# A fused attention, gMLP and expert-attention kernel: the order of all work replaced, with fewer warm-up and filler products

## The chip, the cores and the metric

The kernel runs on one core of one Trainium2 chip. The metric is the device time of one launch in microseconds (us). A core has five engines that matter here: PE (TensorE) for products, DVE (VectorE), ACT (ScalarE) and POOL (GpSimd) for everything element by element, and SP (SyncE), from which this kernel issues every transfer (DMA). Each engine works through its own list of instructions in order; an instruction waits until what it reads is there and the buffer that it writes is free.

## What is computed

The reference, cut to what matters (B=4 batches, H=8 heads, S=576 positions, D=64, so 512 wide; E=4 experts):

```
def _attn_ref(q, k, v):                      # sliding window of 64
    scores = q @ k.T / sqrt(D), masked to 0 <= i - j < 64
    return softmax(scores) @ v
def _moe_ref(x, w_in, w_spatial, b_spatial, w_out):
    h = np.maximum(x @ w_in, 0.0)            # 512 -> 1024
    u, v = h[..., :512], h[..., 512:]
    v_n = (v - mu) / np.sqrt(var + 1e-06)
    v_s = np.einsum('ts,bsd->btd', w_spatial, v_n) + b_spatial
    return (u * v_s) @ w_out
def _moe2_ref(x, w_gate, wq, wk, wv, wo):    # the two best of 4 experts a position
    logits = x @ w_gate; topk, w = best two, softmax over them
    for e in range(E):
        q, k, v = x @ wq[e], x @ wk[e], x @ wv[e]
        ye = softmax(causal(q @ k.T / sqrt(Hd))) @ v @ wo[e]
        out += (weight of e in the best two, or 0) * ye
    return out
```

The result is `_moe2_ref(_moe_ref(_attn_ref(q, k, v)))`.

## The kernel before, in words

All matrices are split in two parts, a head (`xh`, `wh`, `qk`'s first half) and the rest (`xl`, `wl`), and a product of two matrices is three products of parts, so that nearly every result that PE leaves in PSUM is read twice: once by a copy to the head (line 415 on DVE, line 411 on ACT, through `copy`) and once by a subtraction for the rest (`sub`, line 424, on DVE or POOL).

Phase 1 runs the first two stages. `s_mm` (line 624) makes the window scores of two heads of a batch, DVE masks them (line 647), ACT takes the exponential (line 654), the probabilities are turned (`p_t`, line 681) or go through memory, and `pv` multiplies them by v. `prep64` (line 775) splits the loaded w_in in several steps on ACT, DVE and POOL; `b_v` (line 1017) and `b_u` (line 1096) multiply by its two halves, `b_mix` (line 1112) mixes positions. w_out is folded into wq, wk and wv (`prep_w2`, line 1266). Phase 2, from about 244 us, runs the experts in two pairs (`pr` 0 and 1) for each batch: `c_qk` (line 1430) makes q and k of a pair, the tile `qk` holds their heads and rests, `c_gate` (line 1512) picks the two best experts with 15 small operations on DVE (lines 1538 to 1552), scores are masked on DVE (lines 1641 and 1686), `c_pv` (line 1751) multiplies by v, `c_wo` (line 1798) by wo, and the output is stored.

Every piece of work is a node of a `Planner` (line 176). A node has a number, the engines on which it may run with a planned duration for each, and the nodes and buffers that it needs. Two tables fix everything: `ORDER` lists the node numbers in the order in which they are written into the program, and `ON` gives a digit for each, the engine (0 PE, 1 ACT, 2 DVE, 3 POOL, 4 SP). `run` walks the tables, so the planned durations, the start times in `free` and the landing of a DMA in `start` no longer decide anything once the tables stand; they served the search that made the tables. PSUM is a ring of 8 banks, and SBUF tiles are rings too, so a node can also wait for a buffer.

Two kinds of node compute nothing that is used: node 0 is a run of `WARM` products of a 128x128 tile of zeros, `hot`, at the start, and nodes 1 to 60 are fillers, one such product each, of which the tables list some. [...]

```
    warm = r_mm.new()
    def heat(n):
        for _ in range(n):
            mm(warm[:, :128], hot, hot)
    a = N((PE, 427.0 * WARM), lambda e: heat(WARM), alloc=[warm], prio=-1e9)
    for _ in range(FILL):
        N((PE, 228.0), lambda e: heat(1), [a], use=[warm], prio=1e9)
```

Of the kernel before, what the change touches and what calls it, by code (L numbers as in the profile page):

```python
# [1926 lines left out]
```

## Time and profile before

| | |
|---|---|
| median of 3 runs | 411.7 us (409.5 to 412.14) |
| the profiled execution | 408.59 us, of which the profile's span is 406.8 us |
| PE busy | 390.8 us, 96% of the span |
| DVE busy | 333.2 us, 82% |
| ACT, POOL busy | 208.8 and 209.9 us, 51 and 52% |
| moved by DMA | 72.45 MB, 178 GB/s on the mean |

Durations below come from the one profiled execution, which was 3.1 us faster than the median of the runs. An engine that is busy at nearly all times bounds the kernel only in the stretches in which the others wait for it, so the table is to be read together with the busy time by stretch.

### The profile page before, as it was taken

How to read it: one execution, taken by the hardware profiler on the slowest of the kernel's cores; microseconds unless marked ns; L12 is line 12 of the kernel's file. 1: busy time of each engine (PE TensorE's matmuls, PEld its weight loads, DVE VectorE, ACT ScalarE, POOL GpSimd, SP SyncE). 2: the span in 40 equal slices, each digit the busy share in tenths (PEclk: the TensorE clock that was granted, in tenths of full speed). 3: DMA queues.
4: the chain of work that ended last, by engine and by line, in shares of the span. 5: the costliest groups of instructions: out<-in, count | busy, mean ns of one | idle time of the engine just before them, and what ended most of it. 6: DMA issues, size and time to landing. Idle time of an engine off the chain costs nothing.

```text
span 406.8 us, 10676 instructions
## 1 busy us (share of the span) xinstructions
PE 390.8 (96%) x3678; PEld 346.3 (85%) x3678; DVE 333.2 (82%) x1213; ACT 208.8 (51%) x708; POOL 209.9 (52%) x278
## 2 busy tenths in 40 slices
PE   8798898999999999999999999999899989999996
PEld 7676688998799989998999999999689968896765
DVE  5998799879889868758747685899999999998852
ACT  4999786955296574321222141483573346354332
POOL 7787697455279545526371765355742255122400
PEclk9999999999999999999999999999999999999999
DMA  7999769679695855450220110028775977899874
GB/s 270 290 348 314 236 157 302 202 217 271 174 341 150 235 151 155 121 161 12 76 75 3 26 54 2 1 45 230 190 180 128 263 166 210 250 278 252 234 225 129
DMA packets 88410, 72.45 MB, mean 178 GB/s; under 512 B 15138, under 2 KB 80418, under 8 KB 88356
## 3 DMA queue, kind: packets, MB, share of 16 engines
q1 hardware_dynamic: 88356, 71.77, 61.3%
q8 instruction: 29, 0.48, 0.5%
q14 instruction: 25, 0.20, 0.1%
HBM read 47.89 MB, written 23.86 MB: 176 GB/s over the span
## 4 chain that ended last, share of the span: by engine, by line
PE 64%; DVE 23%; DMA 6%; ACT 3%; issue 3%; SPq 1%; POOL 0%; DVEq 0%; ACTq 0%
PE bank L400 63%; DVE p L1641 2%; DVE pa L647 2%; DVE p L1656 2%; DVE p L1686 2%; ACT pa L654 1%; DVE qk L424 1%; DMA qa<-in_qT_dram 1%; DMA d<-p 1%; SPq L506 1%; DMA pg<-d 1%; DMA kt<-in_kT_dram 1%; DMA dr<-pa 1%; DVE p L1653 1%; DVE pa L702 1%
## 5 line engine op out<-in xcount | busy, mean ns | idle before, releaser
L400 PE MATMUL bank<-xh,w 128*128 128x288 f32 x512 | 106.8, 296 | 0.4 <-DVE xl L424 0.4
L400 PEld LDWEIGHTS bank<-xh,w 128*128 128x128 f32 x512 | 83.5, 188 | 2.2 <-DVE xl L424 0.7
L400 PE MATMUL bank<-xl,w 128*128 128x288 f32 x256 | 75.4, 294 | 0.0
L400 PE MATMUL bank<-w,xh 128*128 128x512 f32 (+1 forms) x256 | 64.6, 342 | 0.1
L1653 POOL TENSOR_SCALAR p<-p,mg,fx 128x256 f32<-128x256 f32 (+3 forms) x45 | 27.7, 624 | 42.6 <-DVE ga L1539 10.0
L400 PEld LDWEIGHTS bank<-xl,w 128*128 128x128 f32 x256 | 48.1, 188 | 0.4
L400 PEld LDWEIGHTS bank<-w,xh 128*128 128x128 f32 x256 | 42.7, 188 | 5.2 <-ACT xh L411 0.3
L400 PE MATMUL bank<-w,xl 128*128 128x512 f32 (+1 forms) x128 | 43.3, 338 | 0.9 <-DVE xl L424 0.9
L1645 ACT ACTIVATE p<-p,mg 128x128 f32<-128x128 f32 (+3 forms) x56 | 30.9, 553 | 18.9 <-DVE mg L1641 10.6
L654 ACT ACTIVATE pa<-pa,mp 128x128 f32<-128x128 f32 x96 | 37.2, 391 | 2.2 <-issue 2.0
L647 DVE CUSTOM_DVE_ANT_0 pa<-bank,mask 128x128 f32<-128x128 f32 x120 | 28.4, 283 | 4.2 <-PE bank L400 4.1
L400 PE MATMUL bank<-qk 64*128 64x320 f32 (+4 forms) x288 | 27.7, 329 | 2.5 <-DVE qk L424 2.0
L400 PEld LDWEIGHTS bank<-qk 64*128 64x128 f32 x288 | 22.0, 185 | 6.8 <-ACT xh L411 1.8
L400 PEld LDWEIGHTS bank<-w,xl 128*128 128x128 f32 x128 | 24.1, 188 | 4.0 <-DVE xl L424 1.3
L1072 POOL TENSOR_TENSOR st<-st,nhalf 128x1 f32<-128x1 f32 (+1 forms) x20 | 14.2, 715 | 24.7 <-DVE st L1070 19.3
L1641 DVE CUSTOM_DVE_ANT_0 p<-bank,kmask 128x128 f32<-128x128 f32 (+3 forms) x56 | 25.1, 482 | 0.5
L424 POOL TENSOR_TENSOR vl<-vr,vh 128x512 fp32r<-128x512 f32 x14 | 19.2, 1374 | 11.0 <-ACT vh L411 10.7
L400 PE MATMUL bank<-pg,v 128*64 128x128 f32 (+2 forms) x224 | 23.9, 354 | 1.0 <-DVE qk L424 1.0
L400 PE MATMUL bank<-wsp_h,vh 128*128 128x288 f32 x80 | 24.0, 301 | 0.3 <-DVE mp L647 0.3
L400 PE MATMUL bank<-wsp_h,vl 128*128 128x288 f32 x80 | 23.6, 295 | 0.0
L400 PE MATMUL bank<-wsp_l,vh 128*128 128x288 f32 x80 | 23.6, 294 | 0.0
L1656 DVE STREAM_TRANSPOSE p<-p 128x768 f32<-128x768 f32 (+1 forms) x21 | 22.2, 1057 | 0.9 <-POOL p L1653 0.8
(277 smaller groups left out, 1053.6 us busy)
## 6 DMA issues: line engine op xcount, KB each, us to landing
vt<-in_v_dram SPq DMA_DIRECT2D x12, 512.0 KB, 5.8
dr<-pa SPq DMA_DIRECT2D x64, 96.0 KB, 3.1
pt<-dr SPq DMA_DIRECT2D x16, 384.0 KB, 4.7
d<-p SPq DMA_DIRECT2D x56, 96.0 KB, 2.0
qa<-in_qT_dram SPq DMA_DIRECT2D x44, 96.0 KB, 5.3
out_dram<-ot SPq DMA_DIRECT2D x15, 256.0 KB, 3.6
y<-in_w_in_dram SPq DMA_DIRECT2D x7, 512.0 KB, 6.3
d<-p SPq DMA_DIRECT2D x28, 128.0 KB, 3.0
```

Of the source, the lines that this page charges most:

```text
L400: pe.matmul(o, lhsT, rhs, start=start, stop=stop)
L424: engs[e].tensor_tensor(out=o, in0=a, in1=hi.bitcast(F32), op=ALU.subtract)
L506: nc.sync.dma_start(o, i)
L647: dve.tensor_tensor_reduce(out=at(j, e2), in0=sq(ps[:, j * 128:(j + 1) * 128]), in1=sq(mask(j)), scale=-0.125, scalar=3.0e38, op0=ALU.add, ...
L654: act.activation(at(j, e2), at(j, e2), AF.Exp, bias=mx[:, j, 0:1], scale=-1.0, accum_out=mx[:, j, 1:2])
L702: a = N((DVE, 902), lambda e: dve.transpose(pa.t, pa.t), [a], use=[pa], prio=prio, sbuf=True)
L1072: a = N((POOL, 560), lambda e: pool.tensor_tensor(out=st[:m, 9:10], in0=st[:m, 8:9], in1=nhalf[:m], op=ALU.pow), [n1], use=[st])
L1641: a = N((DVE, t_tt(L)), lambda _, ps=ps, c0=c0, L=L, I=I, e=e, n=n: dve.tensor_tensor_reduce(out=put(I, e), in0=as4(ps[:, c0:c0 + L]), in1 ...
L1645: done.append(N((ACT, 284 + 0.87 * L), lambda _, I=I, e=e, n=n: act.activation(put(I, e), put(I, e), AF.Exp, bias=mg[:, n, 0:1], scale=-1. ...
L1653: done.append(N({POOL: 328 + 0.832 * L, DVE: 190 + 0.52 * L}, lambda en, n=n, I=I, e=e: engs[en].tensor_scalar(put(I, e), put(I, e), mg[:, ...
L1656: a = N((DVE, 100 + 4.16 * w), lambda e: dve.transpose(P[:, :4 * w], P[:, :4 * w]), done, use=[P], prio=prio, sbuf=True)
L1686: dve.tensor_tensor_reduce(out=P[HALF[y], i * 320:(i + 1) * 320], in0=ps[y][HALF[y], :320], in1=tmask[HALF[y], 2 * i:2 * i + 2].rearrange( ...
```

## The change

`ORDER` and `ON` are replaced as a whole. The new order lists 1989 nodes, the old one 1996; the seven that are gone are fillers (11 before, 4 after), and `WARM` goes from 7 to 4. What PE multiplies is otherwise the same. By counting the nodes of the tables: 57 go from POOL to DVE, 39 from DVE to POOL, 66 from ACT to DVE, 64 from DVE to ACT, 18 from POOL to ACT and 16 from ACT to POOL; DVE has 871 nodes instead of 851, POOL 220 instead of 240, ACT 352 as before. The numbers of the planner that change with it (durations, start times, landings) do not reach the chip by themselves.

The diff, cut to its core (the first line of `ORDER` stands for both tables):

```diff
-WARM = 7
+WARM = 4
 ORDER = (
-    0, 12, 35, 61, 188, 62, 65, 58, 60, 189, 208, 196, 209, 21, 242, 241, 216, 298, 11, 78, 3, 190, 191, 192, 243, 197, 264, 244, 263, 85, 71, 210,
...
+    61, 0, 54, 27, 24, 62, 242, 65, 188, 208, 189, 241, 243, 263, 196, 264, 299, 209, 71, 298, 78, 68, 190, 191, 192, 64, 197, 216, 244, 265, 198, 251,
...
-        self.nodes, self.free, self.prio = [], [700.0, 2000.0, 2900.0, 7600.0, 560.0], 0.0
-        self.moved, self.data, self.cold, self.unit = [-1e9] * self.FLIGHT, 0.0, 5000.0, 0
+        self.nodes, self.free, self.prio = [], [1050.0, 2000.0, 2900.0, 7600.0, 560.0], 0.0
+        self.moved, self.data, self.cold, self.unit = [-1e9] * self.FLIGHT, 0.0, 1000.0, 0
...
-                self.moved.append(self.data + 250.0 + min(self.BEHIND, 1.2 * (self.data - t - self.WAY)))
+                self.moved.append(self.data + 450.0 + min(self.BEHIND, 1.2 * (self.data - t - self.WAY)))
...
-        S_N[n0] = S_N[n0 + 1] = top = N((PE, 654), s_mm, kn + [Q_N[n0], Q_N[n0 + 1], S_N.get(n0 - 1)], alloc=bank, use=hk, prio=prio,
+        S_N[n0] = S_N[n0 + 1] = top = N((PE, 680), s_mm, kn + [Q_N[n0], Q_N[n0 + 1], S_N.get(n0 - 1)], alloc=bank, use=hk, prio=prio,
...
-        n2 = N_(155, lambda: tt(out=gt(), in0=lf, in1=le, op=ALU.is_gt), [n1])
+        n2 = N_(270, lambda: tt(out=gt(), in0=lf, in1=le, op=ALU.is_gt), [n1])
```

Planned durations are also raised for the other gate operations, the power on POOL (560 to 680), two small operations of `b_v` and of the scores, one kind of `b_v` product and `c_pv` (651 to 760).

PE at the start of the program; a row is a line, an operation, what it writes and reads, its shape and how often it follows itself. `hot` is the tile of zeros, `vt` holds q and k of the first heads, a `bank` is one of PSUM's eight:

```order
 L1923 UNCONDITIONAL_BRANCH
-L400 MATMUL bank_68<-hot 128x128 x9
+L400 MATMUL bank_68<-hot 128x128 x7
 L400 MATMUL bank_69<-vt 64x128
 L400 MATMUL bank_70<-vt 64x128
```

Two products fewer stand ahead of the first scores; two between the first and the second scores, three behind the second and four further on are gone too, and one stands ahead of the first turned probabilities.

SP at the start, before (`in_w_in` is the weight w_in, whose loads to `prep64` go into `y`; `in_qT`, `in_kT` and `in_v` are what the attention reads):

```order
L506 DMA vt<-in_kq_dram 128x768 x2
L506 DMA ut_164<-in_kT_dram 128x4x256
L506 DMA qa<-in_qT_dram 128x192 x3
L506 DMA y_240<-in_w_in_dram 128x1024
L506 DMA qa<-in_qT_dram 128x192 x2
L506 DMA y_268<-in_w_in_dram 128x1024
L506 DMA y_270<-in_w_in_dram 128x1024
L506 DMA qa<-in_qT_dram 128x192
L506 DMA ut_164<-in_kT_dram 128x4x192
```

And in the change:

```order
L506 DMA y_248<-in_w_in_dram 128x1024
L506 DMA ut_164<-in_kT_dram 128x4x192
L506 DMA wol<-in_v_dram 128x2x256
L506 DMA qa<-in_qT_dram 128x192 x3
L506 DMA woh<-in_v_dram 128x2x256
L506 DMA qa<-in_qT_dram 128x192
L506 DMA kt<-in_kT_dram 128x576
L506 DMA woh<-in_v_dram 128x3x256
L506 DMA kt<-in_kT_dram 128x576
L506 DMA qa<-in_qT_dram 128x192 x2
L506 DMA y_479<-in_w_in_dram 128x1024
```

The first row of this is the second load of w_in and the last its third, which had stood next to the second: nine rows of the attention's loads have moved ahead of it. The later loads of w_in move back in the same way.

DVE where q and k of batch 1, second pair, are split, before (`qk_3464` is the tile of that pair; line 424 takes the rest of one piece out of its bank; `p`, `mc` are score tiles and their sums, `ga`, `gb` the gate's):

```order
L424 TENSOR_TENSOR qk_3464<-bank_72,qk_3464 128x288
L1686 ISA p_3474,mc_3457<-bank_69,tmask 64x320
L1686 ISA mc_3457 64x1
L1686 ISA p_3474,mc_3457<-bank_73,tmask 64x320
L1686 ISA mc_3457 64x1
L1546 TENSOR_REDUCE gb_3454<-ga_3453 128x20
L1691 TENSOR_REDUCE mc_3457<-mc_3457 128x1
L1699 STREAM_TRANSPOSE p_3472<-p_3472 128x640
L424 TENSOR_TENSOR qk_3464<-bank_75,qk_3464 128x288
L424 TENSOR_TENSOR ol_3483<-bank_71,oh_3477 128x256
L424 TENSOR_TENSOR qk_3464<-bank_70,qk_3464 128x288
```

And in the change, where that pair's tile is `qk_3459` and `qk_3461` is that of the first pair:

```order
L424 TENSOR_TENSOR qk_3461<-bank_75,qk_3461 128x288
L1656 STREAM_TRANSPOSE p_3469<-p_3469 128x768
L1547 TENSOR_SCALAR gb_3449<-gb_3449 128x20
L424 TENSOR_TENSOR qk_3461<-bank_68,qk_3461 128x288
L424 TENSOR_TENSOR qk_3459<-bank_69,qk_3459 128x288
L1694 TENSOR_SCALAR mc_3451<-mc_3451 128x1
L1656 STREAM_TRANSPOSE p_3468<-p_3468 128x768
L424 TENSOR_TENSOR qk_3461<-bank_71,qk_3461 128x288
L1695 RECIPROCAL mc_3451<-mc_3451 128x1
L1548 TENSOR_TENSOR fx_3447<-fx_3447,gb_3449 128x20
L424 TENSOR_TENSOR qk_3459<-bank_73,qk_3459 128x288
L424 TENSOR_TENSOR qk_3459<-bank_72,qk_3459 128x288
```

Both pairs of batch 1 are now split close to one another, and the last two pieces of the second pair follow each other with no work between. On PE all scores of the first pair now stand between the products of the second pair and its scores. Over all of phase 2 the copies to the head of `qk` are 4 on DVE and 28 on ACT, where they were 11 and 21.

## Rows read from the trace of the kernel before

**Rows 1.** The page: busy time by engine, and the chain that ended last.

```profile
PE 390.8 (96%) x3678; PEld 346.3 (85%) x3678; DVE 333.2 (82%) x1213; ACT 208.8 (51%) x708; POOL 209.9 (52%) x278
PE 64%; DVE 23%; DMA 6%; ACT 3%; issue 3%; SPq 1%; POOL 0%; DVEq 0%; ACTq 0%
```

**Rows 2.** Busy time by stretch; length, busy us (instructions), granted clock, DMA share, GB/s.

```profile
0.00:10.00 10.00, 8.56 (x100) 7.51 (x100) 5.09 (x38) 4.29 (x17) 7.16 (x37) 1.00 0.78 267
10.00:20.00 10.00, 7.66 (x130) 5.94 (x132) 10.00 (x58) 10.00 (x43) 7.64 (x10) 1.00 0.95 293
20.00:30.00 10.00, 9.62 (x150) 7.69 (x144) 9.72 (x58) 9.65 (x42) 8.85 (x11) 1.00 1.06 356
30.00:40.00 10.00, 8.98 (x118) 7.04 (x110) 8.12 (x33) 9.05 (x36) 7.33 (x9) 1.00 0.98 312
...
120.00:260.00 140.00, 140.00 (x1200) 132.62 (x1200) 103.29 (x281) 50.24 (x148) 74.01 (x86) 1.00 0.33 93
...
280.00:300.00 20.00, 18.31 (x168) 16.11 (x165) 19.29 (x73) 11.77 (x34) 9.53 (x12) 1.00 0.84 218
...
320.00:340.00 20.00, 18.25 (x153) 16.36 (x152) 18.68 (x67) 9.80 (x31) 10.93 (x14) 1.00 0.84 227
...
0.00:91.20 91.20, 82.44 (x1069) 70.49 (x1070) 77.19 (x378) 71.30 (x284) 64.58 (x96) 1.00 0.84 260
```

**Rows 3.** What PE waited for, 0 to 100 us: in total, times, longest.

```profile
PE bank L400 <- DVE ut L421: 1.4, 1, 1.4
...
PE bank L681 <- DVE y L828: 1.0, 2, 0.7
PE bank L400 <- DVE y L828: 1.0, 1, 1.0
```

**Rows 4.** Timeline of PE at the start: start, duration, instructions.

```profile
1.05 4.21 PE L400 MATMUL bank<-hot 128*128 128x128 f32 x18 [1.05 <-DVE hot L432]
5.19 1.28 PE L400 MATMUL bank<-vt 64*64 64x128 f32 x24
...
7.05 0.89 PE L400 MATMUL bank<-vt 64*64 64x128 f32 x24
...
13.87 1.06 PE L400 MATMUL bank<-hot 128*128 128x128 f32 x8
```

**Rows 5.** Timeline of PE around two scores of phase 2, waits in brackets.

```profile
287.90 0.30 PE L400 MATMUL bank<-xl,w 128*128 128x288 f32 x1
288.04 0.30 PE L400 MATMUL bank<-xh,w 128*128 128x288 f32 x1
288.26 1.58 PE L400 MATMUL bank<-pg,v 128*64 128x128 f32 x24
...
290.48 1.91 PE L400 MATMUL bank<-qk 64*128 64x128 f32 x17 [0.29 <-DVE qk L424]
293.77 0.94 PE L400 MATMUL bank<-qk 64*128 64x320 f32 x8 [1.38 <-DVE qk L424]
...
330.33 0.88 PE L400 MATMUL bank<-pg,v 128*64 128x128 f32 x12 [0.95 <-DVE qk L424]
331.66 0.41 PE L400 MATMUL bank<-qk 64*128 64x320 f32 x2 [0.45 <-DVE qk L415]
332.43 1.25 PE L400 MATMUL bank<-qk 64*128 64x320 f32 x16 [0.35 <-DVE qk L424]
```

**Rows 6.** Timeline of DVE: its first operation on scores.

```profile
6.66 0.29 DVE L647 CUSTOM_DVE_ANT_0 pa<-bank,mask 128x128 f32<-128x128 f32 x1 [3.67 <-PE bank L400]
```

**Rows 7.** Timeline of DVE: two operations of the gate.

```profile
286.25 1.47 DVE L1539 TENSOR_TENSOR ga<-lg 128x80 f32<-128x80 f32 x1
...
326.08 1.21 DVE L1550 TENSOR_SCALAR gb<-gb 128x5 f32<-128x5 f32 x1
```

**Rows 8.** Copies to the head of `qk`: ns min/median/max, first and last start.

```profile
L411 ACT ACTIVATE qk<-bank x21: 387/408/414, 243.7 to 363.7; 128x288 fp32r<-128x288 f32 x21
L415 DVE CAST qk<-bank x11: 394/449/458, 248.3 to 366.6; 128x288 fp32r<-128x288 f32 x11
```

More of the change, by code (lines that the diff above doesn't have):

```diff
@@ L115 @@
[L115 to L118 removed]
+    "40000444002404244244441224122022013212312222401202312423401204214224442022123120012323300122411240023230014122422223203011112221"
@@ L119 @@
+    "00242232124122422012232012112224121210221022422242132203123222014212202144204320222230221220244102402421312222222222141122011202"
+    "22222221102440112212442322314033232120242101012022200012412422122210231212212224304342122222023101200012211124220224402222220041"
+    "221223004101102201144222002412240201222142224012202202401414014020414"
 )
@@ L1068, in b_v @@
         a = N((DVE, 600), lambda e: dve.bn_stats(st[:m, 0:6], vr[:m]), [a], alloc=[st], use=[vs])
-        a = N((DVE, 70), lambda e: dve.bn_aggr(st[:m, 6:8], st[:m, 0:6]), [a], use=[st])
+        a = N((DVE, 100), lambda e: dve.bn_aggr(st[:m, 6:8], st[:m, 0:6]), [a], use=[st])
         n1 = N((DVE, 70), lambda e: dve.tensor_scalar(st[:m, 8:9], st[:m, 7:8], 1e-6, None, op0=ALU.add), [a], use=[st], sbuf=True)
         n2 = N((DVE, 70), lambda e: dve.tensor_scalar(st[:m, 10:11], st[:m, 6:7], -1.0, None, op0=ALU.mult), [a], use=[st], sbuf=True)
-        a = N((POOL, 560), lambda e: pool.tensor_tensor(out=st[:m, 9:10], in0=st[:m, 8:9], in1=nhalf[:m], op=ALU.pow),
+        a = N((POOL, 680), lambda e: pool.tensor_tensor(out=st[:m, 9:10], in0=st[:m, 8:9], in1=nhalf[:m], op=ALU.pow),
               [n1], use=[st])
@@ L1537, in c_gate @@
         tt, tr_ = dve.tensor_tensor, dve.tensor_reduce
[L1538 to L1542 removed]
+        n1 = N_(200, lambda: tr_(out=m1(0), in_=lg, axis=AX.X, op=ALU.max), LG_N[b], [ex, ga, gb])
@@ L1543, in c_gate @@
+        n2 = N_(270, lambda: tt(out=gt(), in0=lf, in1=le, op=ALU.is_gt), [n1])
+        n3 = N_(270, lambda: tt(out=eq(), in0=lf, in1=le, op=ALU.is_equal), [n1])
+        n4 = N_(200, lambda: tt(out=ex.t, in0=lg, in1=lead(0), op=ALU.subtract), [n1])
+        n3 = N_(270, lambda: tt(out=eq(), in0=eq(), in1=lowpair[:, None, :, :].to_broadcast(sh), op=ALU.mult), [n3])
         n4 = N((ACT, 210), lambda e: act.activation(ex.t, ex.t, AF.Exp), [n4], use=[ex])
         nf = N_(0, lambda: None, [n2, n3, n4])
-        n2 = N_(155, lambda: tt(out=gt(), in0=gt(), in1=eq(), op=ALU.add), [n2, n3])
@@ L1546, in c_gate @@
-        n2 = N_(150, lambda: tr_(out=rk(), in_=gt(), axis=AX.X, op=ALU.add), [n2])
-        n2 = N_(80, lambda: dve.tensor_scalar(rk(), rk(), 1.5, None, op0=ALU.is_lt), [n2])
-        n2 = N_(90, lambda: tt(out=ex.t, in0=ex.t, in1=rk(), op=ALU.mult), [n2, n4])
-        n2 = N_(90, lambda: tr_(out=m1(1), in_=ex.t, axis=AX.X, op=ALU.add), [n2])
-        n2 = N_(70, lambda: dve.tensor_scalar(m1(1), m1(1), 1e-9, None, op0=ALU.add), [n2])
-        n2 = N_(75, lambda: dve.reciprocal(m1(1), m1(1)), [n2])
@@ L1552, in c_gate @@
-        n4 = N_(90, lambda: tt(out=ex.t, in0=ex.t, in1=lead(1), op=ALU.mult), [n2])
-        n4 = N_(70, lambda: dve.tensor_copy(ex[HALF[1], 4, 0:NE:2], ex[HALF[1], 4, 1:NE:2]), [n4])
+        n2 = N_(270, lambda: tt(out=gt(), in0=gt(), in1=eq(), op=ALU.add), [n2, n3])
+        n2 = N_(260, lambda: tr_(out=rk(), in_=gt(), axis=AX.X, op=ALU.add), [n2])
+        n2 = N_(160, lambda: dve.tensor_scalar(rk(), rk(), 1.5, None, op0=ALU.is_lt), [n2])
+        n2 = N_(200, lambda: tt(out=ex.t, in0=ex.t, in1=rk(), op=ALU.mult), [n2, n4])
@@ L1554, in c_gate @@
+        n2 = N_(200, lambda: tr_(out=m1(1), in_=ex.t, axis=AX.X, op=ALU.add), [n2])
+        n2 = N_(160, lambda: dve.tensor_scalar(m1(1), m1(1), 1e-9, None, op0=ALU.add), [n2])
+        n2 = N_(160, lambda: dve.reciprocal(m1(1), m1(1)), [n2])
+        n4 = N_(200, lambda: tt(out=ex.t, in0=ex.t, in1=lead(1), op=ALU.mult), [n2])
+        n4 = N_(160, lambda: dve.tensor_copy(ex[HALF[1], 4, 0:NE:2], ex[HALF[1], 4, 1:NE:2]), [n4])
         n1 = nf
@@ L1596, in scores @@
                 ps = [r_sc.new(), r_sc.new()]
-                a = N((PE, 3 * t_mm(320)), lambda _, ps=ps, i=i: three([p[:, :320] for p in ps], (S - 64, S - 128), tail(i)),
+                a = N((PE, 3 * t_mm(320) + 25), lambda _, ps=ps, i=i: three([p[:, :320] for p in ps], (S - 64, S - 128), tail(i)),
                       deps + ns + [QK_N[b, pr, "pad"]], alloc=ps + ([] if i else [P, mc] + gets), use=[qk], prio=prio, form=3)
@@ L1647, in far @@
         m = len(todo)
-        a = N((DVE, 72), lambda _: dve.tensor_scalar(mg[:, :m, 3], mg[:, :m, 2], 1e-9, None, op0=ALU.add), done, use=[mg], prio=prio)
+        a = N((DVE, 140), lambda _: dve.tensor_scalar(mg[:, :m, 3], mg[:, :m, 2], 1e-9, None, op0=ALU.add), done, use=[mg], prio=prio)
         a = N((DVE, 67 + 8 * m), lambda _: dve.reciprocal(mg[:, :m, 3], mg[:, :m, 3]), [a], use=[mg], prio=prio)
@@ L1779, in c_pv @@
         cs = slice(i0, i0 + 256)
-        o = N((PE, 651 if grp == 0 else 2056), go, PG_N[b, pr, grp] + V2_N[b] + (VT_N[b] if grp else []) + ([] if new else O_N[b, pr][:1]),
+        o = N((PE, 760 if grp == 0 else 2056), go, PG_N[b, pr, grp] + V2_N[b] + (VT_N[b] if grp else []) + ([] if new else O_N[b, pr][:1]),
               alloc=[ps] + new, use=[pg, v2] + ([vt] if grp else []), prio=prio, form=2)
```

34 lines of the change are left out of this document (13 added, 21 removed), and 124 rows, old and new, of the table ORDER.

## The prediction

> **What bounds the kernel now.** I read the page first, then the busy time by stretch, then the waits of PE, then the timeline at the places named. On the page PE is busy 390.8 of 406.8 us, and it also holds 64% of the chain of work that ended last, DVE 23% [rows 1]. So the sum can come down in two ways only: PE gets less to do, or PE's idle 16.0 us shrink. Busy time by stretch tells where those lie [rows 2]. From 120 to 260 us PE is busy 140.00 of 140 us: whatever is reordered there changes nothing but PE's own work. The idle time is in the first 100 us (1.44 + 2.34 + 0.38 + 1.02 us in the first four stretches of 10 us alone), where DVE is busy 10.00 and 9.72 of 10 us and ACT about as much, and in two stretches of phase 2 (1.69 us in 280 to 300, 1.75 us in 320 to 340), where DVE is busy 19.29 and 18.68 of 20 us. PE's waits agree: early ones on DVE's weight and score work, up to 1.4 us each [rows 3]; late ones on DVE's splitting of q and k, 1.38 us the longest [rows 5]. The change is a new order, so its worth is: which of these waits go, and which new ones come.
>
> **The start.** PE began with 18 records of the `hot` product (7 warm products and 2 fillers, two records each), 4.21 us from 1.05, and the first scores followed at 5.19 [rows 4]. The change has 7 products there, 14 records. At 4.21 / 18 = 0.23 us that is four records, 0.9 us; from the start of one to the next it is a little less, about 0.21 us, so 0.85 us. The data is no hindrance: DVE's first operation on scores waited 3.67 us for PE alone [rows 6], and the scores' two loads, the first in SP's queue before and after, are ahead of everything. But the first 24 score records took 1.28 us, the next 24 0.89 [rows 4]: PE worked at its lower rate until some of them were done, though the stretch is written with a granted clock of 1.00 [rows 2]. Starting earlier, the first scores run wholly at the low rate and need some 0.15 us more. DVE and ACT are the full engines afterwards, so they start 0.7 us earlier: **-0.7** (0 if a load further on sets the pace, -0.85 at most). Of the nine fillers that stood further on one is left. The last four of them, eight records at 13.87, took 1.06 us [rows 4] while DVE was full and PE had nothing ready. I cost the removal of these eight at nothing: what hides it is the wait for DVE, and where that cover is gone the removal is a gain, not a loss.
>
> **The rest of the first 91 us.** Up to the first `b_v` of batch 1 (91.2 us) DVE was busy 77.19 us [rows 2]. Giving each instruction ahead of that product in the new order its own duration in the trace of before, DVE has 3.3 us less to do by then, ACT 0.9 less, POOL 4.2 more, PE 2.2 less. That bounds the gain at -3.3, since DVE is on the chain there. Against it stand the loads: SP issues all of them in order, and adding up the loads in SP's order, the fourth load of w_in for `b_v` ends after 7,328 KB instead of 5,856. 1,472 KB are 1.5 MB, at the 356 GB/s of 20 to 30 us [rows 2] 4.2 us. The last load of the `b_u` half ends 992 KB later, 1.0 MB, 3.3 us at 312 GB/s. Behind each load stand the splitting on ACT, DVE and POOL, in order, with other work queued behind it; how much slack it had the rows do not tell. Ends: -3.3 and +4.2; I take **-0.6**, near the middle of the two (0.45), a little to the side of the gain because DVE is the fuller engine.
>
> **Scores of batch 1, second pair of experts.** At 290.48 and 293.77 PE waited 0.29 and 1.38 us for the low halves of q and k [rows 5]. DVE was late: a gate operation of 1.47 us stood in its queue at 286.25 [rows 7]. The new order puts about 6.6 us of PE work between the last `c_qk` product of this pair and its scores, where 3.8 us stood. 2.8 us of cover is more than 1.67 us of wait: **-1.5** (0 to -1.67). Also seven of eleven casts of q and k leave DVE for ACT (0.449 us each [rows 8], 3.1 us in all), which on ACT take 0.408 us. ACT has room: 11.77 of 20 us busy in 280 to 300 [rows 2].
>
> **Scores of batch 2, second pair.** The waits were 0.95, 0.45 and 0.35 us [rows 5], 1.75 in all, behind the gate of batch 2 (one operation of 1.21 us [rows 7]). Here the PE work between product and scores goes from 4.6 to 4.3 us, no better, but the three casts that stood in DVE's run here go to ACT (1.3 us), and gate operations now stand between the subtractions. Ends 0 and -1.75; I take **-0.5**.
>
> **Changes of tile shape.** PE's start-to-start time in one shape was 0.14 us (287.90 to 288.04) and 0.22 us where the next product used another shape (288.04 to 288.26) [rows 5]: 0.08 us for a change. Counted node by node, the order has 86 such changes instead of 95: nine times 0.08 is 0.7 us, ends 0 and -0.8 with some of them dearer. About half falls where PE is the bound: **-0.4**.
>
> **New waits.** An order with 20 more nodes on DVE must wait somewhere. Where I can see a thinner cover: scores of batch 1's first pair, now directly behind their split (0 to 1.4 us, the size of the waits of [rows 5]), and the tail, where `c_wo` products of batches 1 and 2 were gathered ahead of the last softmax, and the last `c_pv` is followed after 0.8 us of PE work, not 2.2, by the `c_wo` that needs its split (0.2 to 0.8). Ends 0 and +4 (three waits of the longest kind); I take **+1.0**.
>
> **Sum.** -0.7 - 0.6 - 1.5 - 0.5 - 0.4 + 1.0 = -2.7 us. Against the profiled execution (408.59 us with its 1.8 us outside the span) 405.9; the median of the runs is 411.7, so 409.0.
>
> **Rivals.**
> A. The waits only move. DVE is busy 96% of 280 to 300 us and 93% of 320 to 340 [rows 2], the new order hands it 57 nodes of POOL's and gives back 39, and each late split there waits behind something. Then new waits are +3.5 rather than +1.0 and the time is 411.5. For it: DVE's share; against it: the casts that leave DVE, and 36.7 idle us of DVE in 120 to 260 [rows 2], where added work is free.
> B. All of it comes: -0.85, -3.3, -1.67, -1.75, -0.8 and +1.0 give -7.4, so 404.3. For it: each place is named in the waits; against it: the loads, at 293 to 356 GB/s through the first 40 us already [rows 2].
> C. Slower: the weights come late. If the fourth `b_v` load and the last `b_u` load both arrive late by their 4.2 and 3.3 us with no slack, PE waits 7.5 us in 25 to 50 us; with the -2.1 of the other terms it is +5.4, 417. It decides once the lateness passes about 6.2 us; the mechanism is one queue, SP, in order. Against it: PE has other work in between, and two loads late do not usually add.
> D. PE's rate falls back. Fewer `hot` products leave PE idle more from 6 to 16 us. Its first records took 0.23 us each, later ones 1.06 / 8 = 0.13 [rows 4]: 1.77 times as long. [...] Against it: with 7.66 of 10 us busy the stretch from 10 to 20 us kept a granted clock of 1.00 [rows 2], and no wait in the first 100 us was over 1.4 us [rows 3]. [...]
>
> **How the numbers follow.** Forecast 0.50 (405 to 411), A 0.22, B 0.16, C 0.08, D 0.04. 1% is about what a measurement of this kernel tells from no change, 4.1 us: faster means under 407.6. Of the forecast two fifths lie there, with B 0.20 + 0.16 = 0.36; slower is C and D, 0.12; the rest, 0.52, is the same. The range 403.3 to 413.5 leaves out C, D and a part of B's low side, under 0.2 together; the forecast's own range is 405 to 411.
>
> **What would show it.** Right: DVE's first operation on scores at about 6.0 instead of 6.66; no wait over 0.5 us at the scores of batch 1's second pair; PE busy about 387 to 389; granted clock 1.00 throughout. Wrong: waits of PE on `w` or on the splitting of w_in between 25 and 50 us (C), a granted clock under 1 there (D), waits on DVE in 260 to 380 us of more than 3.5 us in all (A).

## The result, and the profile after

The change takes 412.69 us (median of 16 runs, 411.09 to 414.76), the kernel before, on the same chip, 409.82 us (16 runs, 407.52 to 412.19). The ratio is 1.0062, 95% interval 1.0037 to 1.0087: slower by 0.6%. That is under the 1% which the prediction called a change, but it is clear of zero and on the other side than the forecast, which was 2.7 us faster. The base of the forecast, 411.7 us from three runs, was itself 1.9 us high, so the time 409.0 missed by 3.7 us and the difference by 5.6.

Before any experiment, what the trace of the change says. The profiled execution took 413.74 us, its span 411.9. It is 1.1 us above the median of the change, and the one of the kernel before, 408.59 us, 1.2 us below its own, so the two traces stand 5.2 us apart and the medians 2.9. First the page: busy time by engine, PE's granted clock by fortieths of the span, and the chain that ended last.

```profile
PE 390.9 (95%) x3658; PEld 348.5 (85%) x3658; DVE 345.4 (84%) x1235; ACT 207.9 (50%) x713; POOL 193.6 (47%) x256
...
PEclk9699996999999999999999999999999999999999
...
PE 52%; DVE 24%; DMA 11%; SPq 4%; ACT 3%; issue 3%; POOL 1%; DVEq 0%; ACTq 0%; POOLq 0%
```

Against [rows 1]: PE is busy as long as before with 20 records fewer (two for each of the ten products of `hot` that are gone), DVE 12.2 us longer, and PE's share of the chain fell from 64 to 52%. The clock has two dents, one in the second fortieth and one in the seventh (62 to 72 us), which the profile of the kernel before does not show. Next, busy time by stretch of the change, columns as in [rows 2].

```profile
10.00:20.00 10.00, 6.54 (x85) 5.40 (x85) 7.62 (x46) 8.10 (x35) 5.73 (x8) 0.72 0.97 311
...
60.00:80.00 20.00, 16.89 (x177) 15.39 (x176) 19.45 (x67) 13.56 (x50) 15.68 (x16) 0.83 0.82 230
...
120.00:260.00 140.00, 135.56 (x1158) 127.45 (x1157) 110.97 (x290) 47.53 (x144) 68.44 (x76) 1.00 0.34 99
...
120.00:140.00 20.00, 18.56 (x205) 17.13 (x203) 17.68 (x51) 12.12 (x48) 15.29 (x14) 1.00 0.74 210
...
220.00:240.00 20.00, 18.31 (x145) 18.11 (x144) 14.97 (x31) 4.74 (x9) 9.31 (x10) 1.00 0.05 14
240.00:260.00 20.00, 18.69 (x150) 18.49 (x149) 17.14 (x48) 3.92 (x11) 7.28 (x12) 1.00 0.08 28
280.00:300.00 20.00, 19.88 (x181) 18.72 (x180) 19.57 (x73) 8.82 (x27) 12.94 (x18) 1.00 0.82 206
...
320.00:340.00 20.00, 18.97 (x157) 16.11 (x157) 19.27 (x64) 8.45 (x28) 12.16 (x15) 1.00 0.77 207
```

Two things happened at once. In phase 2 the idle time that the prediction spoke of went: PE is busy 19.88 instead of 18.31 us in 280 to 300 and 18.97 instead of 18.25 in 320 to 340. In phase 1 idle time came up where there was none: 4.44 us in 120 to 260, where PE had been busy 140.00 of 140 us [rows 2] (1.44 us of it in 120 to 140, 1.69 in 220 to 240, 1.31 in 240 to 260), and 3.11 us in 60 to 80, where the kernel before had 1.63, as its own row shows:

```profile
60.00:80.00 20.00, 18.37 (x207) 17.32 (x206) 18.20 (x73) 16.19 (x66) 12.47 (x11) 1.00 0.83 250
```

PE's waits in the change name who was late (in total, times, longest, us), over the whole span:

```profile
PE bank L400 <- DVE ut L421: 4.5, 2, 2.8
PE bank L400 <- DMA qa<-in_qT_dram: 4.4, 2, 2.3
...
PE bank L400 <- DVE w L424: 1.3, 1, 1.3
```

And the timeline of PE in the change shows where (start, duration, instructions, the wait in brackets):

```profile
8.06 1.54 PE L400 MATMUL bank<-ut,qa 64*64 64x128 f32 x48 [2.29 <-DMA qa<-in_qT_dram]
...
15.12 2.95 PE L400 MATMUL bank<-ut,qa 64*64 64x128 f32 x48 [2.15 <-DMA qa<-in_qT_dram]
...
67.08 1.91 PE L400 MATMUL bank<-kt,qa 64*64 64x128 f32 x24 [2.83 <-DVE ut L421]
...
223.09 0.51 PE L400 MATMUL bank<-w,pa 128*128 128x256 f32 x2 [1.69 <-DVE ut L421]
...
252.90 0.39 PE L400 MATMUL bank<-w,xh 128*128 128x260 f32 x1 [1.31 <-DVE w L424]
...
300.82 1.40 PE L400 MATMUL bank<-qk 64*128 64x128 f32 x18
...
336.83 0.79 PE L400 MATMUL bank<-qk 64*128 64x320 f32 x6 [0.70 <-DVE qk L424]
```

The first two waits are for loads of q. The wait of 2.83 us is for DVE to empty a bank into `ut` (line 421) and stands between `b_u` and the mixing of batch 0; that of 1.69 us at 223.09 is the same line, far on; that of 1.31 us at 252.90 is the folding of w_out into the experts' weights (line 1312). From 260 us to the scores of batch 2 no score waits any more, those at 300.82 among them; those of batch 2 wait 0.70 us.

Why was DVE late at 67? Its timeline in the change (first row: the first operation on scores, to be compared with [rows 6]):

```profile
5.29 0.29 DVE L647 CUSTOM_DVE_ANT_0 pa<-bank,mask 128x128 f32<-128x128 f32 x1 [2.30 <-PE bank L400]
...
62.49 3.33 DVE L424 TENSOR_TENSOR t2w<-y,t2w 1x576 fp32r<-1x576 f32 x1
65.83 0.75 DVE L424 TENSOR_TENSOR t2w<-y,t1w 64x576 fp32r<-64x576 f32 x1
...
218.45 2.53 DVE L415 CAST vh<-vr 128x512 fp32r<-128x512 f32 x1 [1.56 <-PE bank L400]
```

The same subtraction in the kernel before:

```profile
63.85 0.77 DVE L424 TENSOR_TENSOR t2w<-y,t2w 1x576 fp32r<-1x576 f32 x1
```

And POOL in the change, at the time of the 3.33 us:

```profile
61.84 0.77 POOL L1074 TENSOR_SCALAR pa<-pa,st 64x512 f32<-64x512 f32 x1
62.58 1.40 POOL L424 TENSOR_TENSOR wsp_l<-y,wsp_h 128x576 fp32r<-128x576 f32 x1
63.94 1.26 POOL L424 TENSOR_TENSOR vl<-vr,vh 128x512 fp32r<-128x512 f32 x1
```

One operation of DVE took 3.33 instead of 0.77 us; it began while POOL worked through three operations in a row and ended 0.62 us after the last of them. POOL's run seems to have held it. That is a reading of two timelines, which do not show why; m1 and m4 below test what it is worth. It is no accident of one execution: in the traces of e1 and f1 below, which have the change's order there, the same subtraction took 3.33 and 3.35 us.

### The profile page after: what moved, and what is told of

Read it like the earlier page. It is cut to its first block, busy times and chain, and to the rows that moved or that the text cites. A ratio compares the mean times of both kernels' runs of the same rounds, so it can differ in the third digit from the quotient of the medians.

```text
span 411.9 us, 10648 instructions
## 1 busy us (share of the span) xinstructions
PE 390.9 (95%) x3658; PEld 348.5 (85%) x3658; DVE 345.4 (84%) x1235; ACT 207.9 (50%) x713; POOL 193.6 (47%) x256
## 4 chain that ended last, share of the span: by engine, by line
PE 52%; DVE 24%; DMA 11%; SPq 4%; ACT 3%; issue 3%; POOL 1%; DVEq 0%; ACTq 0%; POOLq 0%
PE bank L400 51%; SPq L506 4%; DMA pg<-d 4%; DMA d<-p 3%; DVE pa L647 3%; DVE p L1641 2%; DMA qa<-in_qT_dram 2%; DVE p L1656 1%; DVE vl L424 1%; DVE p L1686 1%; DVE xl L424 1%; DVE st L1068 1%; DVE w L424 1%; DVE pa L702 1%; ACT pa L654 1%
## 5 line engine op out<-in xcount | busy, mean ns | idle before, releaser
L1653 POOL TENSOR_SCALAR p<-p,mg,fx 128x512 f32<-128x512 f32 (+3 forms) x44 | 27.5, 637 | 52.2 <-ACT p L1645 11.6
L1645 ACT ACTIVATE p<-p,mg 128x512 f32<-128x512 f32 (+3 forms) x56 | 30.9, 555 | 22.6 <-issue 11.3
L1072 POOL TENSOR_TENSOR st<-st,nhalf 128x1 f32<-128x1 f32 (+1 forms) x20 | 12.3, 618 | 28.4 <-DMA dr<-pa 12.1
L1641 DVE CUSTOM_DVE_ANT_0 p<-bank,kmask 128x512 f32<-128x512 f32 (+3 forms) x56 | 25.1, 483 | 0.6 <-issue 0.2
L400 PE MATMUL bank<-kt,qa 64*64 64x128 f32 x432 | 18.8, 294 | 3.1 <-DVE ut L421 2.8
```

The lines of the kernel that those rows point to most:

```text
L400: pe.matmul(o, lhsT, rhs, start=start, stop=stop)
L1072: a = N((POOL, 680), lambda e: pool.tensor_tensor(out=st[:m, 9:10], in0=st[:m, 8:9], in1=nhalf[:m], op=ALU.pow), [n1], use=[st])
L1641: a = N((DVE, t_tt(L)), lambda _, ps=ps, c0=c0, L=L, I=I, e=e, n=n: dve.tensor_tensor_reduce(out=put(I, e), in0=as4(ps[:, c0:c0 + L]), in1 ...
L1645: done.append(N((ACT, 284 + 0.87 * L), lambda _, I=I, e=e, n=n: act.activation(put(I, e), put(I, e), AF.Exp, bias=mg[:, n, 0:1], scale=-1. ...
L1653: done.append(N({POOL: 328 + 0.832 * L, DVE: 190 + 0.52 * L}, lambda en, n=n, I=I, e=e: engs[en].tensor_scalar(put(I, e), put(I, e), mg[:, ...
```

## The experiments

Times are medians in us; ratios are to the kernel before measured beside each kernel.

### The start: fillers and the clock

In the change the granted clock stood at 0.72 on the mean of 10 to 20 us and the 48 score records at 15.12 took 2.95 us. Theory 1: the missing fillers cost the time (rival D). Theory 2: the loads set the pace there, and PE's rate hardly counts. The first kernel is the change with sixteen fillers more, eight in each of the two waits (the old tables had seven more than the change).

```diff
 # e1_after_fill: ORDER of the change
-... 208, 189, ... 214, 252, ...
+... 208, (8 fillers), 189, ... 214, (8 fillers), 252, ...
```

> The changed kernel with 16 fillers put back, eight after the first two scores and eight after the first three turned probabilities; nothing else differs. Theory 1 (PE's idle time of 2.29, about 1.3 and 2.15 us between 5.8 and 15.1 us let its clock fall to 0.50 from 14.8 to 21.5 us, and PE is then the bound): granted clock 1.00 from 10 to 30 us, the products after 15 us at half their length (0.89 instead of 1.5 us for 24 score records), time 2 to 3 us under the changed kernel, about 410 us if that is at 412.7. Theory 2 (DVE, ACT and the loads of q set the pace in this stretch, and PE's rate is hidden): the clock comes back but the time stays within 0.5 us of the changed kernel.

In this trace the clock was up. Busy time by stretch of this kernel, then its timeline of PE:

```profile
10.00:20.00 10.00, 8.63 (x158) 7.35 (x160) 9.63 (x63) 9.94 (x43) 7.08 (x10) 1.00 1.04 332
```

```profile
14.62 1.63 PE L400 MATMUL bank<-ut,qa 64*64 64x128 f32 x48
```

The records took 1.63 instead of 2.95 us at a clock of 1.00. One trace does not prove that the fillers did it (m3 below, without them, shows 1.00 there too), but the executions agree: their mean clock was 0.990 to 0.999 with the fillers, 0.982 to 0.996 without. The subtraction of `t2w` that stood at 62.49 us began 2.7 us earlier in that trace, at 59.80. Yet the time was 411.94 (10 runs, 410.5 to 412.97), ratio 1.0064 (1.0035 to 1.0093): 0.75 us less than the change by the medians, and by the ratio as far over the kernel before as the change is. What e1 still loses against the kernel before shows behind the start: its trace has PE idle for 1.39 us in 120 to 140, 1.69 in 200 to 220 and 1.31 in 240 to 260, the change's three waits. The second kernel asks the same from the other side.

```diff
 # e2_before_nofill: ORDER of the kernel before
-(the nine fillers behind the first two)
```

> The kernel before without the nine fillers that stand after the first scores (the 7 warm-up products and two fillers at the start stay). Theory 1: the granted clock falls under 1 somewhere in 10 to 25 us and the kernel is 1.5 to 3 us slower than before. Theory 2: the clock stays, or falls where PE is not the bound: within 0.5 us of before.

Its busy time by stretch:

```profile
10.00:20.00 10.00, 7.90 (x108) 6.58 (x109) 9.90 (x57) 9.39 (x41) 7.74 (x10) 0.69 0.95 302
```

The clock fell to 0.69 on the mean of the stretch, and the time was 409.27 (10 runs), ratio 1.0001 (0.9967 to 1.0035). The low clock of rival D came, and the time stayed within the interval's 0.35%, 1.4 us: DVE was busy 9.90 of 10 us. Theory 2, within that.

### Which phase

Theory A: phase 1 loses and phase 2 gains. Both tables are cut where phase 1 ends (before: 1156 entries, change: 1149) and joined crosswise.

```diff
 # h1_p1before_p2after; ON in the same way
-ORDER = before
+ORDER = before[:1156] + change[1149:]
 # h2_p1after_p2before
-ORDER = before
+ORDER = change[:1149] + before[1156:]
```

> The tables of before up to the last node of phase 1 (1156 entries), those of the change from there on. By the two traces the first product of q in phase 2 starts 5.9 us later in the change and its end is 5.1 us later, so phase 2 gains about 0.8 us. Theory A (the whole loss is in phase 1): 0.5 to 2.5 us faster than before, 407.5 to 409.3. Theory B (phase 2 of the change lives from a late start, since work that it needs has piled up ready): no gain, or up to 1.5 us slower than before.

> The tables of the change up to the last node of phase 1, those of before from there on. Theory A: 4 to 6 us slower than before, 414 to 416. Theory B: 2 to 3 us slower, like the change itself.

h1 took 405.72 (10 runs, 404.89 to 407.61), ratio 0.9896 (0.9867 to 0.9926); it beats both kernels. h2 took 415.52 (4 runs), ratio 1.015 (1.0089 to 1.0211). So phase 2 of the change is worth 1.0%, about 4.3 us, and its phase 1 costs 1.5%, about 6 us; 1.5 less 1.0 is the 0.6 of the change within the intervals. A stretch of phase 2 of h1, whose phase 2 begins 7.6 us before that of the change:

```profile
280.00:300.00 20.00, 20.00 (x183) 18.73 (x183) 19.63 (x77) 12.46 (x42) 9.32 (x15) 1.00 0.86 216
```

PE is never idle there.

### Where in phase 1

A ladder: the change's list up to a point, then what is left of phase 1 in the order and on the engines of the kernel before, then always the change's phase 2. The names say up to which time of the change's trace.

```diff
 # s_a54: k = 334; s_a84: k = 469; s_a200: k = 974
-ORDER = change
+ORDER = change[:k] + (what is left of before[:1156], no fillers) + change[1149:]
```

> The other way round: phase 1 in the order and on the engines of the change up to its node 330 (about 54 us), then before's order for what is left of phase 1, then the change's phase 2. Up to 55 us the change had done 1.0 us more useful work on PE than before, by the two traces. Theories P and S: 404.5 to 407 (P) or 407.1 (S). Theory B: 410 or more.

> Phase 1 in the order and on the engines of the change up to its node 465 (about 84 us), then before's for what is left of phase 1, then the change's phase 2. The same with the switch at 54 us took 407.1. If the change loses 3 us or more in 60 to 75 us (wait of 2.8 us and a clock of 0.50 to 72 us): 409 to 411. If nothing is lost there: 406.5 to 407.5.

> The same with the switch at node 970 of phase 1 (about 200 us in the change), so that of the change's phase 1 only its last 50 us are replaced. The last 50 us cost 3.8 us when they were put behind before's order (409.5 against 405.7). If they cost the same here: 3 to 4 us under the change's 412.7, 408.7 to 409.7. If they only cost there because of the seam: 411.5 or more.

| the change's order up to | time | ratio (interval) | step |
|---|---|---|---|
| 0 us (h1) | 405.72 | 0.9896 (0.9867 to 0.9926) | |
| 54 us (s_a54) | 407.09 | 0.9953 (0.9927 to 0.9979) | +0.57% |
| 84 us (s_a84) | 410.92 | 1.0041 (1.0017 to 1.0066) | +0.88% |
| 200 us (s_a200) | 408.37 | 0.9988 (0.9959 to 1.0017) | -0.53% |
| all of phase 1 | 412.69 | 1.0062 (1.0037 to 1.0087) | +0.74% |

A cut has a price of its own, since work on its two sides was not ordered for each other (s_a54 has a wait of 2.9 us for ACT that neither kernel has, and by the expectation above PE in the change was not behind at 55 us), so a step can be off by that. Two steps stand out: 54 to 84 us, 3.6 us, and the last 50 us of phase 1, 3.0 us. The first is too large: right behind its cut s_a84 has PE idle for 3.03 us in 84 to 120, where the change has none.

```profile
84.00:100.00 16.00, 15.52 (x162) 12.95 (x161) 13.26 (x61) 9.26 (x45) 8.42 (x7) 1.00 0.73 216
100.00:120.00 20.00, 17.45 (x216) 15.12 (x215) 17.60 (x68) 9.04 (x26) 9.84 (x12) 1.00 0.75 230
```

That idle time is gone in s_a200, where the ladder falls again by 0.53%. Safer is the sum over the cut: up to 200 us the change's order costs 0.92%, 3.8 us, and the last 50 us cost 3.0. Part of the 3.8 us lies in 60 to 80 us, as two rows show, that of s_a54 first, then that of s_a84:

```profile
60.00:80.00 20.00, 18.45 (x207) 17.40 (x206) 18.01 (x71) 16.70 (x68) 11.75 (x11) 1.00 0.77 231
```

```profile
60.00:80.00 20.00, 16.87 (x199) 14.96 (x201) 19.16 (x63) 12.68 (x49) 11.94 (x11) 0.91 0.79 233
```

The ladder from the other side, the kernel before first:

```diff
 # s_b50: k = 306; s_b83: k = 481; s_b195: k = 976
-ORDER = change
+ORDER = before[:k] + (what is left of change[:1149], no fillers) + change[1149:]
```

> Phase 1 in the order and on the engines of before up to its node 295 (about 50 us), then the change's order for what is left of phase 1, then the change's phase 2. Theory P (the loss lies in 60 to 75 us, where the change puts the mixing products of batch 0 ahead of attention work): as slow as the change, 411.5 to 413. Theory S (the loss is spread evenly over phase 1, 6.9 us from the hybrid's 405.7 to the change's 412.7): 1.4 us under the change, 411.3. Theory B (it lies at the start): 405.7 to 407.

> The same with the switch at node 470 of phase 1 (about 83 us in the kernel before). Theory P: 3 to 4 us under the change, 408.5 to 409.5, since what is left is the loss after 120 us (idle PE of 1.4 us in 120 to 140, 1.7 and 1.3 us in 220 to 260). Theory S: 410.3. Theory B: 405.7 to 407.

> The same with the switch at node 965 of phase 1 (about 195 us). Left of the change's phase 1 are its last 50 us, with the waits of 1.7 us at 223 and 1.3 us at 253. Theory P: 408 to 409. Theory S: 407. Theory B: 405.7.

s_b195 took 409.5 (10 runs), ratio 1.0007 (0.998 to 1.0034): with the change's order in the last 50 us alone, h1 loses 1.1%, which agrees with the step of 0.74%. s_b50 took 416.02 (4 runs), ratio 1.0162, and s_b83 416.47 (4 runs), ratio 1.0163: both slower than the change itself, so what they show is their cut (in s_b83 a wait of 2.7 us for a load of q), and by their times they locate nothing. Their traces agree with the ladder, though: s_b50, with the change's order from 50 us on, has PE busy 16.98 of 20 us in 60 to 80, s_b83, with the old order there, 18.36.

### The three waits, mended one by one

Theory L: the operation on DVE named by a wait makes the loss, or only hands it on; theory M: PE's wait goes with it. m1 moves the two subtractions of `t2w` on DVE behind three banks that PE needs.

```diff
 # m1_t2w_later: DVE's list
+L421 ut<-bank_74
-L424 t2w<-y,t2w 1x576
-L424 t2w<-y,t1w 64x576
 L700 mp
-L421 ut<-bank_74
 L421 ut<-bank_70
 L421 ut<-bank_68
+L424 t2w<-y,t2w 1x576
+L424 t2w<-y,t1w 64x576
```

> The changed kernel with one thing moved: DVE does the two subtractions of the last rows of the spatial weight (written to t2w, line 424) behind three operations that free PE's banks (line 421, written to ut), not ahead of them. In the changed kernel the first of the two, over one partition only, took 3.33 us from 62.49, until POOL's run of three operations from 61.84 to 65.20 had ended; PE waited 2.83 us for ut and its clock was at 0.50 from 66 to 72 us. Theory K (a DVE operation between SBUF tiles that meets a run of POOL operations is held until the run ends, and what is queued behind it waits with it): t2w is still long or starts when the run is over, but PE's wait at 67 us goes to under 0.5 us, the clock stays 1.00 from 60 to 80 us, and the kernel is 3.5 to 5 us faster than the changed one, about 408 to 409. Theory L (DVE is busy 19.45 of 20 us in 60 to 80 anyway, so whatever is put first, PE waits as long a little later): under 1 us faster.

412.73 (10 runs), ratio 1.0048 (1.002 to 1.0076): nothing gained. The wait moved, as the timeline of PE in m1 shows:

```profile
67.01 1.29 PE L400 MATMUL bank<-kt,qa 64*64 64x128 f32 x24 [2.05 <-DVE mp L647]
...
69.51 0.61 PE L400 MATMUL bank<-xh,w 128*128 128x288 f32 x1 [1.21 <-DVE mp L647]
```

m2 does the like at 223 us, one row of DVE ahead of the cast of 2.53 us; m3 gives four casts of the folding (nodes 1185, 1197, 1200 and 1203, line 1312) from DVE to ACT, which had 3.92 us of work in 20 there.

```diff
 # m2_ut_ahead: DVE's list
+L421 ut<-bank_75
 L415 vh<-vr
 L1074 pa
-L421 ut<-bank_75
 # m3_fold_on_act: ON, nodes 1185, 1197, 1200, 1203
-2 (DVE)
+1 (ACT)
```

> The changed kernel with one DVE operation (line 421, the ut that frees a bank for the product at 223.09) moved ahead of the cast of vh that took 2.53 us at 218.45. Theory K: the wait of 1.7 us on that ut goes, and PE is busy 20.00 of 20 us in 220 to 240. Theory L: PE waits for something else on DVE within the next 10 us, more than 1 us in all.

> The changed kernel with four casts of the folded weight (line 1312, 0.41 us each, bound between 246 and 251 us) on ACT instead of DVE. Theory M (DVE is the bound from 241 to 253 us, since the change gave it casts that ACT had before, 9 on DVE and 7 on ACT instead of 4 and 14): PE's wait of 1.31 us at 252.90 falls to under 0.3 us. Rival: the wait stays, since the chain at its end runs through the weight's own subtraction of 1.21 us.

One run each. m2: 412.0; the wait of 1.69 us became one of 1.5 us for ACT (line 419). m3: 409.81; the wait at 252.90 is gone, and PE is busy 19.77 instead of 18.69 us in that stretch of it:

```profile
240.00:260.00 20.00, 19.77 (x159) 19.57 (x158) 14.97 (x49) 5.15 (x16) 6.51 (x12) 1.00 0.02 8
```

All three edits in one kernel:

```diff
 # m123_all
+m1_t2w_later + m2_ut_ahead + m3_fold_on_act
```

> The three moves together. If each gives what its own wait is, 4 to 5 + 1.7 + 1.3 us: 7 to 8 us under the changed kernel, 404.5 to 406, which is 1% under before. Theory L: the waits come back as others on DVE, 409 or more.

410.66 (10 runs), ratio 1.0016 (0.9987 to 1.0045): 2.0 us less than the change where 7 to 8 were expected. What each edit gave of it is not shown; m1 alone gave nothing, m2 and m3 have one run each. m4 then takes the two subtractions away from DVE altogether:

```diff
 # m4_t2w_on_pool: m123_all, and ON of t2w's two subtractions
-2 (DVE)
+3 (POOL), and both eight entries later in ORDER
```

> The kernel with the three moves together, and the two subtractions for t2w on POOL instead of DVE, so that DVE meets no run of POOL with them (on DVE they took 2.54 and 0.75 us when moved, 0.74 and 0.77 in the kernel before). Theory K (the hold is what DVE lacks in 60 to 70 us): PE's waits on DVE between 62 and 70 us, 3.3 us with the moves alone, fall under 1.5 us, the first copy of q and k on ACT comes 2 us earlier than 247.1, and the time is 408 to 409. Theory L (phase 1's order has more work ahead of this place than DVE and POOL can do, whoever does it): within 1 us of the three moves, 410 to 411.5.

410.88 (10 runs), ratio 1.0051 (1.002 to 1.0082), no better than m123. Its busy time in the stretch, then PE's timeline:

```profile
60.00:80.00 20.00, 16.59 (x167) 14.67 (x166) 15.51 (x64) 13.63 (x51) 18.29 (x17) 0.83 0.81 241
```

```profile
70.66 0.40 PE L400 MATMUL bank<-wsp_h,vl 128*128 128x288 f32 x1 [1.13 <-POOL vl L424]
...
72.08 0.61 PE L400 MATMUL bank<-wsp_h,vh 128*128 128x288 f32 x1 [1.02 <-ACT vh L411]
```

DVE was idle for over 4 us and PE still lost 3.4 of 20 us: now it waited for POOL and ACT. So the subtraction of 3.33 us is not by itself the loss: DVE, POOL and ACT all prepare these products, and with one relieved PE waited for the others. Why they are late together is not shown. A likely reason is the order on PE: from 53 us to the first mixing product of batch 0 the timeline of the change has 96 attention records, that of the kernel before 168, so the three engines have less of other work on PE to hide behind.

### The clock at 67 us

One thing was still open: with the wait of 2.83 us the granted clock went down, to 0.50 in 67 to 70 us. By stretches of three microseconds, the change:

```profile
64.00:67.00 3.00, 0.25 (x10) 0.00 (x1) 2.99 (x5) 1.01 (x2) 1.21 (x1) 0.75 0.80 226
67.00:70.00 3.00, 2.92 (x44) 2.52 (x46) 3.00 (x12) 2.13 (x7) 1.98 (x3) 0.50 0.79 221
70.00:73.00 3.00, 3.00 (x41) 2.55 (x38) 2.97 (x10) 2.47 (x10) 2.25 (x2) 0.61 0.58 176
```

At 0.50 PE took 1.91 us for 24 score records; 24 of the same shape took 0.89 in the kernel before [rows 4], at a clock of 1.00 [rows 2]. Theory K: this is the loss of 54 to 84 us. Theory Q: DVE, busy 3.00 of 3 us, hands out PE's work there, and a faster PE waits sooner. The kernel keeps PE at work through the wait by doing the scores ahead of it three times.

```diff
 # f1_scores_thrice, s_mm
-            for j in range(3):
+            for j in range(3) if n0 != 24 else (0, 1, 2) * 3:
```

> The change, with the scores product that PE works at 62.66 us (24 records, the last work ahead of its longest wait, 2.83 us at 67.08) done three times over into the same two banks instead of once: 48 records more, about 1.9 us of PE work by its own 0.88 us for 22, in the place where PE only waits. DVE's first operation on these scores stands at 67.83 us, so nothing else is moved. Two theories of why 54 to 84 us of the change's order cost 3.6 us. Theory K (clock): the wait lets PE's clock fall; in 67 to 70 us it was granted 0.50, in 70 to 73 us 0.61, and 72 score and pv records took 4.8 us there that take 2.8 us at the upper level. With the gap down to about 0.9 us the clock stays at 1.00 and some 2.0 us come back: 410.7 us, a ratio of about 1.001 to the kernel before, and the first copy of q and k on ACT at about 248 us instead of 250.1. Theory Q (DVE's queue): DVE was busy 2.99 of 3 us in 64 to 67 and 3.00 in 67 to 70, and what PE does in this stretch is handed out by DVE; a faster PE only waits for DVE sooner. Then the clock is 1.00 as well, but new waits of PE of about 2 us in all stand in 67 to 75 us and the time stays that of the change, 412.7 us, a ratio of 1.006. The result is the reference's in both.

413.13 (6 runs, 411.55 to 413.79), ratio 1.0097 (1.007 to 1.0124). In its trace the clock was 1.00 throughout:

```profile
64.00:67.00 3.00, 2.31 (x59) 1.90 (x63) 3.00 (x14) 1.51 (x5) 1.36 (x2) 1.00 0.75 213
67.00:70.00 3.00, 1.89 (x33) 1.65 (x26) 2.97 (x10) 2.49 (x10) 2.25 (x3) 1.00 0.97 310
```

and PE's timeline in it:

```profile
64.69 1.24 PE L400 MATMUL bank<-kt,qa 64*64 64x128 f32 x24 [1.54 <-DVE ut L421]
...
68.71 0.40 PE L400 MATMUL bank<-xh,w 128*128 128x288 f32 x1 [1.11 <-DVE mp L647]
```

The 24 records take 1.24 instead of 1.91 us, and PE waits for DVE instead: 1.11 us at 68.71, 0.40 at 72.79. Theory Q. In that trace DVE's subtraction of `t2w` took 3.35 us. (The execution's clock was 1.00 from the start, and this subtraction began 2.4 us earlier in it than in the change's trace, at 60.09.) That execution took 411.55; the three of the kernel before beside it with a clock of 1.00 took 406.94 to 408.21. So the clock is not what divides the two kernels there.

That does not make the clock free. Of the 106 executions of the kernel before that stand beside the experiments, those with a mean clock of 1.000 took 408.1 us (median of 22), those at 0.990 to 0.992 410.5 (29). The change's sixteen had lower clocks, 0.988 by the median against 0.996. At 0.990 to 0.992 it took 412.0 (5 executions), so at like clocks some 1.5 us of the 2.9 are left, and at 0.995 to 0.996 2.2 (two executions of the change, 38 of the other). Whether the lower clock makes the rest, or the waits make both, is not shown; by the medians e1 and f1, whose profiled executions have a mean clock of 0.996 and 1.000 against the change's 0.983, won 0.75 us and nothing.

### Order or engines

The change replaces two tables. Each was put with the other's, in phase 1 alone, where 163 nodes differ in engine.

```diff
 # x1_order_after_engines_before: ORDER of the change
-ON of the change
+ON of the change, but for phase 1 each node's engine of before
 # x2_order_before_engines_after: ORDER of h1
-ON of h1
+ON of h1, but for phase 1 each node's engine of the change
```

> The change, but every node of phase 1 runs on the engine that it has in the kernel before (163 digits of the second table go back); the order is the change's. Theory E (the engines are the loss: 20 nodes more on DVE, held by POOL): first copy of q and k on ACT at 244 to 246 instead of 250.1, time 406 to 408. Theory O (the order is the loss): within 1.5 us of the change or slower, since the order was fitted to its engines.

> The hybrid with phase 1 of before and phase 2 of the change, but the nodes of phase 1 on the engines that the change gives them. Theory E: 3 us or more slower than the hybrid with its own engines, 409 or more. Theory O: within 1.5 us of it, 404.5 to 407.

433.84 (4 runs), ratio 1.0608, and 426.14 (4 runs), ratio 1.042. Both are far worse than either kernel: order and engines are fitted to each other, and this split cannot say which of the two lost the time. It does say what a table is worth: x1 is 21.2 us slower than the change and x2 20.4 us slower than h1, for the engines of 163 nodes.

## Why the prediction was wrong

**The step that failed** is the sentence on the stretch from 120 to 260 us: "PE is busy 140.00 of 140 us: whatever is reordered there changes nothing but PE's own work". A stretch without waits was taken for one without risk, and the sum has no term for waits there. What keeps it full is its order: h1, with the old order there, has PE busy in all of it, and the new order gave 4.44 us of idle there, 1.44 in 120 to 140, 1.69 at one `ut` and 1.31 at one fold of the weights. It is the larger part of what phase 1 lost, some 6 us (h2); giving the last part of phase 1 alone the change's order costs 0.74 to 1.1% (the ladder, s_b195). Rival A's "36.7 idle us of DVE in 120 to 260, where added work is free" falls with it: DVE was busy 7.7 us more there, and in m3 a wait went when four casts were taken away from DVE.

**The rest of the first 91 us, -0.6 (ends -3.3 and +4.2).** Also wrong. With the start it was forecast to bring the first `b_v` of batch 1 1.3 us earlier; in the traces that product begins 2.6 us later, first before, then the change:

```profile
91.19 0.62 PE L400 MATMUL bank<-w,xh 128*128 128x512 f32 x2
```

```profile
93.79 0.62 PE L400 MATMUL bank<-w,xh 128*128 128x512 f32 x2
```

In e1 and f1, with a clock of 1.00 instead of 0.72 in 10 to 20 us, the subtraction of `t2w` began 2.7 and 2.4 us earlier than in the change, so much of the 2.6 may be the clock of that execution. What stays at a higher clock is the idle time in 60 to 80 us: 3.11 us in the change (clock 0.83), 3.15 in e1 (0.91) and 3.32 in f1 (1.00), where the kernel before has 1.63. The low end was made by giving each of DVE's instructions its duration in the trace of before; in the new order one of them took 3.33 instead of 0.77 us. The high end was put on loads of w_in, and they were not it: the waits are on DVE's `ut` and on q's loads. Together the two failures make 5.9 us of new idle time on PE (1.48 in 60 to 80 and 4.44 behind 120), against gains of some 4 us in phase 2; some 1 us of the 2.9 measured is not placed.

**The start, -0.7.** DVE's first operation on scores came at 5.29 us, earlier than the 6.0 expected [rows 6], and then nothing of it was left: PE waited 2.29 and 2.15 us for loads of q. The end "0 if a load further on sets the pace" seems to have been the case, though no run moved these loads by themselves. **The fillers, at nothing**: right for the kernel before (e2, 1.0001), for the change 0.75 us by the medians, which the intervals do not tell from nothing (e1).

**Rival D**, which I had given 0.04, came true in the clock and not in the time. In the change the clock was 0.72 on the mean of 10 to 20 us and 0.50 in 67 to 70, where the kernel before has 1.00. The range leaves D out as far slower; no run shows such a loss from a low clock there: at 0.69 in 10 to 20 us the kernel before stood at 1.0001 (e2). What makes the clock fall the runs do not settle: m3 has the change's order in 10 to 20 us, with PE busy 7.09 us there against 6.54, and shows 1.00. Putting more fillers back won 0.75 us by the medians (e1), and without the nine DVE was busy 9.90 us in 10 to 20 (e2).

**Scores of batch 1, second pair, -1.5.** Right: waits of 0.29 and 1.38 us [rows 5] are gone. **Batch 2, second pair, -0.5.** Right in kind and small: 1.75 us became 0.70. **New waits, +1.0**: right in phase 2 (0.3, 0.3 and 0.2 us beside the 0.70), far too small for phase 1, where I had priced none behind 91 us. **Changes of tile shape, -0.4**: PE's busy time cannot show it, 390.9 us at a clock that was lower in places (0.72 in 10 to 20 us, 0.83 in 60 to 80). All of phase 2 was forecast at -1.0 us without the tile shapes and measured at -1.04%, some 4 us (h1), so this part was right in sign and too small. PE's waits from 260 us on fell from 3.5 to 1.5 us in the traces; where the other 2 us come from is not shown.

**What stays open.** That the new waits of phase 1 are the loss rests on where they stand and on h1, h2 and the ladder; of the single edits only m3 took a wait away, and m1, m2 and m4 only moved theirs. So no single instruction is the cause. m123 still stands 4.9 us above h1, and its trace has as much more idle time on PE (1.95 us in 60 to 80, 1.48 each in 120 to 140 and 220 to 240, 0.23 in 240 to 260). Why DVE, ACT and POOL are late together there is not explained, and the wait in 120 to 140 was not touched by any run. The price of a cut was not measured by itself.
